# A sequential attention and GLU block on one core: two DMA writes swapped, a QKV tile and an empty background step moved in, transposes of the identity ahead of the first tile

## The chip, the cores and the metric

One core of a Trainium2 chip. The metric is the device time of one execution in microseconds (us), the median of the runs. The engines are named as the profile names them: PE is TensorE's matmul, PEld its weight load, DVE is VectorE, ACT is ScalarE, POOL is GpSimd, SP is SyncE; an engine's name with a q is its instruction queue, which issues DMAs.

## The reference

One sequence of 2048 tokens with 576 features passes a sliding, dilated attention (32 heads of 18, 8 keys at a distance of 2, only backwards) and a gated feed-forward layer, each behind a layer norm and with a residual.

```python
B, S, D, F = 1, 2048, 576, 4608
def attn(x, wqkv, wo):                       # H = 32, Dh = 18, W = 8, dil = 2
    q, k, v = split_heads(x @ wqkv)
    idx = pos[:, None] - arange(W) * dil
    logits = einsum("bhsd,bhswd->bhsw", q, k[idx]) * Dh ** -0.5   # idx < 0: -1e9
    o = einsum("bhsw,bhswd->bhsd", softmax(logits), v[idx])
    return o.reshape(B, S, D) @ wo
def glu(x, w_gate, w_up, w_down):
    return (sigmoid(x @ w_gate) * (x @ w_up)) @ w_down
h = x + attn(layernorm(x), wqkv, wo)
out = h + glu(layernorm(h), w_gate, w_up, w_down)
```

## The kernel before, in words

The tokens are split by parity and halves into four blocks (0 to 3) of 512 tokens, and each block into four tiles of 128. A matrix is held as a rounded part ("hi", made by ACT) and the remainder ("lo", made by DVE from the source and hi), and a product is three matmuls: hi by hi, lo by hi, hi by lo. `split` (lines 104 and 105) makes such a pair; `split_rest` (108 and 109) does it for the last 64 features, which lie twice in one 128-row chunk, so that one matmul takes both parts. Those doubled 64 columns are the "doubled rest": a row of normalised tokens or of attention output is 576 columns and the last 64 once more (`DX` = 640).

The work runs in this order.

- `opening()` takes block 0's first layer norm, its transposes and the QKV product of its first head group. Its instructions on each engine are chained by hand with `ch`: each stands behind the one before it on the same engine. `tr` (L497, L499) transposes a tile on PE by a matmul with the identity; `x_hi` (L504, L505) evicts it on ACT; `x_lo` (L509, L511) makes the remainder on DVE; `w_hi` and `w_lo` (L516, L519) do the same for the weights. `heads_of` runs one QKV tile, which is 14 matmuls of `tok_major` (L157, L159, L160). `qkv_w(1, ...)` splits the second group's weights (tile `qw`, L104 and L105).
- Then the QKV products of the blocks and groups follow on PE, while `att_all`, a generator that is stepped between them, runs the attention of blocks 0 and 1 on DVE (L189 to L226), group by group. Its results for block 0 stay on the chip (tile `tok`); L428 copies their last 64 columns. For other blocks ("spill") POOL writes them to DRAM tensors `o1` to `o3` (L228), and after the last of four groups also the doubled rest (L230), 64 columns for each of 512 tokens against 144 in L228.
- `front()` is block 0's output projection, residual, second layer norm and transposes. It is made of four generators `proj_j`, one a tile, and each `next(fr)` takes all four one step further. Step 1 is `tr_main` (L146) with a split, step 2 `tr_rest` (L150) with `split_rest`, steps 3 and 4 the two halves of the projection with the residual add (L262), then `ln_j` (L123 to L128), and the transposes of the result.
- The main loop runs over 84 items: 12 plain ones (`single`), 24 that take two blocks at once by a seven-product scheme (`pair`), then 12 and 36 for the other half of the tokens. Gate and up products are L746 and L753, down products L864 and L926. Weights come in by SP (L702, tile `wg`) and are split an item ahead (`weights`).
- Between the products of an item, a background generator is stepped by `bg_step`. In the first half it is block 1's projection, in the second the attention of blocks 2 and 3, their projections and the operands of the last pass. `proj_scr` runs such a projection: `load_j` (L707) loads a tile of attention output `oj` and of the input `hj`, then four `proj_j` are taken in turn, one step of one tile at a time, five rounds; their PSUM banks alternate between `b` and `bgp` (`bg_bank`). A plain item offers ten background steps in six places, two of them single and four double or single in turn.

The order on each engine comes from a planner that follows the order of the code, with priorities (`high_priority`). `tc.issue_after(x)` adds that what is issued in its block on x's own engine stands behind x; it sets nothing for other engines and adds no wait. Each engine runs its queue in order.

## Time and profile before

| | |
|---|---|
| runs | 1577.75 us (median), 1576.01 and 1581.7 |
| the profiled execution | 1584.01 us, span 1582.2 us |
| busy in the span | PE 1551.0, DVE 1255.2, ACT 879.2, POOL 199.9 us |
| granted TensorE clock, mean | 0.996 |
| HBM | 143.98 MB read, 130.87 MB written, 174 GB/s over the span |

In the profile's rows a line number is that of the kernel before. A row of a timeline has the start, the duration, the engine, the line, the operation, what it writes and reads, and in brackets the idle time of the engine before it and what ended it. A row of the waits has the total, the number and the longest, in us. Durations of matmuls overlap: the next one begins before the one before has drained. The chain that ended last runs for 58% of the span over PE, for 11% over DVE and for 8% over DMA.

### The profile page before, as it was taken

How to read it: one execution, taken by the hardware profiler on the slowest of the kernel's cores; microseconds unless marked ns; L12 is line 12 of the kernel's file. 1: busy time of each engine (PE TensorE's matmuls, PEld its weight loads, DVE VectorE, ACT ScalarE, POOL GpSimd, SP SyncE). 2: the span in 40 equal slices, each digit the busy share in tenths (PEclk: the TensorE clock that was granted, in tenths of full speed). 3: DMA queues.
4: the chain of work that ended last, by engine and by line, in shares of the span. 5: the costliest groups of instructions: out<-in, count | busy, mean ns of one | idle time of the engine just before them, and what ended most of it. 6: DMA issues, size and time to landing. Idle time of an engine off the chain costs nothing.

```text
span 1582.2 us, 22347 instructions
## 1 busy us (share of the span) xinstructions
PE 1551.0 (98%) x8520; PEld 1377.3 (87%) x8520; DVE 1255.2 (79%) x1883; ACT 879.2 (56%) x1584; POOL 199.9 (13%) x249
## 2 busy tenths in 40 slices
PE   8999999999999999999999999999999999999998
PEld 7999888887888888888888888888888888888887
DVE  6998999969999999999426588866777776677755
ACT  6632244435555645566542355766777766777660
POOL 2300000020000010000101010112112112111210
PEclk9999999999999999999999999999999999999999
DMA  8646445365566677664683524999899989999983
GB/s 284 215 168 220 179 185 190 108 235 183 133 167 170 164 176 192 157 162 109 161 242 125 181 81 126 193 181 177 170 180 186 173 173 181 173 173 186 181 169 120
DMA packets 77147, 273.95 MB, mean 173 GB/s; under 512 B 8336, under 2 KB 14224, under 8 KB 76144
## 3 DMA queue, kind: packets, MB, share of 16 engines
q0 software_dynamic: 28192, 107.29, 37.5%
q1 hardware_dynamic: 41216, 145.11, 27.2%
q10 hardware_dynamic: 7632, 20.12, 3.3%
q8 instruction: 66, 1.08, 0.3%
q14 instruction: 41, 0.34, 0.1%
HBM read 143.98 MB, written 130.87 MB: 174 GB/s over the span
## 4 chain that ended last, share of the span: by engine, by line
PE 58%; issue 16%; DVE 11%; DMA 8%; POOL 4%; ACT 2%; SPq 0%; ACTq 0%; POOLq 0%; DVEq 0%
PE b L746 27%; PE dp L864 13%; PE dp L926 6%; PE b L753 5%; PE acc L157 4%; POOL h L935 3%; DMA wg<-in_wmlp_dram 3%; DVE pr L189 2%; DVE pr L215 1%; DVE lg L193 1%; DVE w L105 1%; DVE pr L221 1%; PE b L157 1%; PE bgp L157 1%; DMA x<-tok 1%
## 5 line engine op out<-in xcount | busy, mean ns | idle before, releaser
L746 PE MATMUL b<-tl,w 128*128 128x512 f32 x1704 | 432.6, 393 | 5.1 <-ACT s L820 3.2
L746 PEld LDWEIGHTS b<-tl,w 128*128 128x128 f32 x1704 | 307.9, 188 | 63.6 <-ACT s L820 4.7
L746 PE MATMUL b<-th,w 128*128 128x512 f32 x1344 | 346.2, 392 | 1.5 <-DVE s L839 1.5
L746 PEld LDWEIGHTS b<-th,w 128*128 128x128 f32 x1344 | 244.8, 188 | 46.5 <-DVE s L839 1.9
L932 ACT ACTIVATE ev<-dp 128x576 f32<-128x576 f32 x224 | 144.7, 646 | 63.2 <-PE dp L926 58.9
L753 PE MATMUL b<-th,w 128*128 128x512 f32 x568 | 175.7, 390 | 0.0
L104 ACT ACTIVATE w<-wg 128x384 fp32r<-128x384 f32 (+1 forms) x186 | 110.8, 601 | 111.1 <-PE b L753 48.8
L935 POOL DMA_DIRECT2D h<-ev x128 | 110.0, 860 | 458.6 <-ACT ev L932 444.7
L157 PE MATMUL acc<-qw,th 128*128 128x432 f32 x512 | 154.3, 362 | 2.5 <-DVE th L109 2.3
L105 DVE TENSOR_TENSOR w<-wg,w 128x640 fp32r<-128x640 f32 (+1 forms) x186 | 120.8, 656 | 41.3 <-ACT w L104 41.1
L105 DVE TENSOR_TENSOR w<-tw,w 128x512 fp32r<-128x512 f32 x120 | 82.6, 688 | 82.1 <-ACT w L104 81.5
L753 PEld LDWEIGHTS b<-th,w 128*128 128x128 f32 x568 | 106.5, 188 | 23.2
L864 PE MATMUL dp<-d,h1h 128*128 128x288 f32 x640 | 119.9, 297 | 0.0
L864 PE MATMUL dp<-d,h0h 128*128 128x288 f32 x608 | 114.1, 297 | 0.8 <-DVE tail L874 0.8
L872 ACT ACTIVATE stage<-dp 128x576 f32<-128x576 f32 x104 | 66.9, 645 | 70.1 <-PE dp L864 69.8
L157 PEld LDWEIGHTS acc<-qw,th 128*128 128x128 f32 x512 | 96.6, 189 | 8.4 <-DVE th L109 3.5
L864 PEld LDWEIGHTS dp<-d,h1h 128*128 128x128 f32 x640 | 99.7, 190 | 3.0
L104 ACT ACTIVATE w<-tw 128x512 fp32r<-128x512 f32 x120 | 75.4, 628 | 46.5 <-PE b L746 40.0
L864 PEld LDWEIGHTS dp<-d,h0h 128*128 128x128 f32 x608 | 95.1, 190 | 4.3 <-DVE tail L874 1.0
L157 PE MATMUL acc<-qw,tl 128*128 128x432 f32 x256 | 92.6, 362 | 0.1
L189 DVE TENSOR_TENSOR pr<-kw,q 128x2304 f32<-128x2304 f32 x32 | 81.8, 2556 | 8.8 <-DMA kw<-k 8.7
L880 POOL DMA_DIRECT2D h<-stage x26 | 31.0, 1194 | 436.3 <-ACT stage L872 350.1
(310 smaller groups left out, 2955.5 us busy)
## 6 DMA issues: line engine op xcount, KB each, us to landing
h<-ev POOLq DMA_DIRECT2D x96, 576.0 KB, 7.1
wg<-in_wmlp_dram SPq DMA_DIRECT2D x47, 928.0 KB, 5.9
h<-stage POOLq DMA_DIRECT2D x26, 1152.0 KB, 9.5
wg<-in_wmlp_dram SPq DMA_DIRECT2D x36, 640.0 KB, 4.3
kw<-k SPq DMA_DIRECT2D x16, 792.0 KB, 5.2
vw<-v SPq DMA_DIRECT2D x16, 792.0 KB, 4.3
wd<-in_wmlp_dram SPq DMA_DIRECT2D x18, 576.0 KB, 7.4
h<-ev POOLq DMA_DIRECT2D x32, 288.0 KB, 6.9
```

The lines of the kernel that those rows point to most:

```text
L104: act.activation(hi, src, AF.Copy)
L105: splits.append(dve.tensor_tensor(lo, src, f32(hi), ALU.subtract))
L157: pe.matmul(ps[:, :n], a[:, c, js], m[:, c], start=k == 0, stop=False)
L189: dve.tensor_tensor(pr, both(kw, u), q[:, us].unsqueeze(2).broadcast_to([P, 2, W, CG]), ALU.mult)
L746: pe.matmul(ps, wt[:, a, k0 + c], xx[:, m + c], start=first and k == 0, stop=k == 5, skip_group_check=True)
L753: pe.matmul(ps, wt[:, a, k0], xx[:, 4], start=False, stop=a == 1, skip_group_check=True)
L864: pe.matmul(ps[:, i, :DH2], a[:, js], d[:, m, i * DH2:(i + 1) * DH2], start=k == 0, stop=k == n)
L872: act.activation(hv, ps, AF.Copy)
L880: pool.dma_start(hacc[b], hs, accum_op=ALU.add, max_dma_last_dim=8 * D)
L926: pe.matmul(ps[:, i, :DH2], a[x][:, js], m[y], start=k in (0, 1, 3) and q == 0, stop=q == 2, skip_group_check=True)
L932: act.activation(hs[:, k % 2], ps[:, :, :DH2], AF.Copy)
L935: pool.dma_start(hsev[:, u, k0:k + 1], hs[:, :k + 1 - k0], accum_op=ALU.add, max_dma_last_dim=8 * D)
```

## The change

Five places are edited.

1. In `attention`, POOL issues the write of the doubled rest ahead of the main write of the same group (last group of a spilled block only).
2. In `qkv_w(1, ...)`, ACT's casts stand behind tile 1's `x_hi` of the opening and DVE's remainders behind tile 1's `x_lo`. Before, one edge on a DVE instruction was given for both.
3. The opening begins with 20 transposes of the identity into a PSUM tile that nobody reads.
4. `front()`'s second step is taken after the third QKV tile of block 2's last group, together with the third step, and no longer right after the first.
5. In `proj_scr` for block 2, the generator yields once without work between the second and third tile of the first round. (A loop variable is renamed there.)

```diff
         if spill:
-            pool.dma_start(oscr[b][:, :, g * CG:(g + 1) * CG], o)
             if g == NG - 1:
                 pool.dma_start(oscr[b][:, :, D:DX], o[:, :, CG - DR:CG])
+            pool.dma_start(oscr[b][:, :, g * CG:(g + 1) * CG], o)
...
-            with ExitStack() as way:
-                way.enter_context(tc.high_priority(HI))
-                if after is not None:
-                    way.enter_context(tc.issue_after(getattr(after, "ins", after)))
-                split(w[:, 0, c], w[:, 1, c], ws)
+            with tc.high_priority(HI):
+                if after is None:
+                    split(w[:, 0, c], w[:, 1, c], ws)
+                    continue
+                x, y = (getattr(a, "ins", a) for a in after)
+                with tc.issue_after(x):
+                    act.activation(w[:, 0, c], ws, AF.Copy)
+                with tc.issue_after(y):
+                    dve.tensor_tensor(w[:, 1, c], ws, f32(w[:, 0, c]), ALU.subtract)
...
         nr, pv, pr = {}, {}, {}
+        pre = mm_tile()
+        for _ in range(20):
+            ch(pe, lambda: pe.transpose(pre[:, :P], ident, ident))
...
             ch(act, lambda: act.activation(th[:, 4, js], pr[j][:, :P], AF.Copy))
+            highs.append(last[act])
...
-    done = opening()
-    w.append(qkv_w(1, None, done[1]))
+    done, highs = opening()
+    w.append(qkv_w(1, None, (highs[1], done[1])))
...
     with tc.issue_after(getattr(last, "ins", last)):
-        for _ in range(2):
-            next(fr)
+        next(fr)
     for b in (2, 3):
         for j, _ in enumerate(more if b == 2 else qkv(b, 3, T[b], w[3])):
             with ExitStack() as way:
                 if (b, j) == (2, 0):
                     way.enter_context(tc.issue_after(getattr(passes[-1], "ins", passes[-1])))
+                    next(fr)
                 next(fr, END)
...
-        for _ in range(5):
-            for gn in live:
+        for k in range(5):
+            for j, gn in enumerate(live):
+                if b == 2 and (k, j) == (0, 2):
+                    yield
                 if todo and n % 2:
-                    j = todo.pop(0)
-                    ins[j][1] = load_j(pj, b, j, 1)
+                    i = todo.pop(0)
+                    ins[i][1] = load_j(pj, b, i, 1)
```

More of the change, by code (lines that the diff above doesn't have):

```diff
@@ L522, in opening @@
         call = qkv(0, 0, T[0], qw)
-        ends = []
+        ends, highs = [], []
         def heads_of(j):
@@ L564, in opening @@
         drain(call)
-        return ends
+        return ends, highs
     w = []
-    done = opening()
-    w.append(qkv_w(1, None, done[1]))
+    done, highs = opening()
+    w.append(qkv_w(1, None, (highs[1], done[1])))
     xb = load_x(1)
```

## The prediction

> **What bounds the kernel now.** I read the page first, then the table of waits of PE, then PE's and DVE's timelines around each long wait, and last a table of stretches for the granted clock.

> ```profile
> span 1582.2 us, 22347 instructions
> PE 1551.0 (98%) x8520; PEld 1377.3 (87%) x8520; DVE 1255.2 (79%) x1883; ACT 879.2 (56%) x1584; POOL 199.9 (13%) x249
> ```

> TensorE works in 98% of the span, so a microsecond is won only where TensorE waits or runs slowly; 1582.2 - 1551.0 leaves 31 us in all. The waits of PE between 180 and 1540 us that this change can touch:

> ```profile
> PE b L146 <- DMA oj<-o: 4.2, 1, 4.2
> ...
> PE b L146 <- DVE tl L105: 2.0, 1, 2.0
> PE mm L150 <- DVE tok L428: 1.7, 1, 1.7
> PE acc L157 <- DVE th L109: 1.6, 1, 1.6
> ```

> In order of time these are: block 0's projection (L428 and L109, near 180 us), block 1's projection (the load oj, at 315 us) and block 2's (L105, at 834 us). Two of them cost more than the wait. The stretches (length, then busy time of PE, PEld, DVE, ACT, POOL; the column after POOL is the granted clock):

> ```profile
> 3.65:14.07 10.42, 7.29 (x30) 5.62 (x30) 9.80 (x26) 7.64 (x18) 3.29 (x7) 1.00 0.97 348
> 181.25:207.20 25.95, 23.76 (x162) 22.96 (x162) 25.32 (x51) 4.66 (x12) 1.38 (x3) 1.00 0.34 134
> ...
> 314.31:317.72 3.41, 0.88 (x6) 0.56 (x4) 1.49 (x2) 1.79 (x3) 0.00 (x0) 1.00 0.18 16
> 317.72:324.55 6.83, 5.13 (x22) 5.08 (x23) 1.50 (x3) 1.55 (x3) 0.00 (x0) 0.50 0.97 364
> 389.40:392.82 3.42, 1.54 (x7) 0.94 (x5) 0.48 (x2) 2.29 (x5) 0.00 (x0) 1.00 0.01 4
> 392.82:396.23 3.41, 2.92 (x12) 2.17 (x12) 3.10 (x6) 2.57 (x5) 0.00 (x0) 1.00 0.00 0
> 833.14:836.55 3.41, 1.46 (x11) 1.09 (x10) 2.99 (x5) 2.83 (x6) 0.00 (x0) 1.00 0.34 83
> 836.55:839.96 3.41, 3.41 (x16) 3.41 (x15) 1.31 (x3) 1.33 (x2) 0.00 (x0) 0.50 0.99 394
> 940.00:1540.00 600.00, 600.00 (x3207) 523.51 (x3206) 440.00 (x757) 418.22 (x736) 111.26 (x129) 1.00 0.87 173
> ```

> After a 3.41 us stretch in which PE was busy for only 0.88 or 1.46 us, the next one or two stretches have half the clock; after one with 1.54 us busy they have not. So the 315 us wait costs 4.23 us and half of 5.13 us of slow work (2.57), and the 834 us wait 1.95 us and half of 3.41 us (1.71). From 940 to 1540 us PE never stops, so what is gained before stays gained.

> [...]

> **The opening: 20 transposes, and ACT's order.**

> ```profile
> 1.16 0.28 POOL masks.py:199 TENSOR_SCALAR_AFFINE_SELECT ident<-ident 128x128 f32<-128x128 f32 x1
> ...
> 6.59 1.12 PE L497 MATMUL mm<-ident,tok 128*128 128x128 f32 x4 [6.59 <-DVE tok L491]
> ...
> 9.78 0.29 ACT L505 ACTIVATE th<-acc 128x128 fp32r<-128x128 f32 x1
> ...
> 9.94 1.15 ACT L104 ACTIVATE qw<-ws 128x432 fp32r<-128x432 f32 x2
> ...
> 13.38 0.69 DVE L509 TENSOR_TENSOR tl<-mm,th 128x512 fp32r<-128x512 f32 x1
> ...
> 14.12 0.19 PEld L157 LDWEIGHTS acc<-qw,tl 128*128 128x128 f32 x1 [0.26 <-DVE tl L509]
> ```

> The identity is ready at 1.44 us. Four transposes take 1.12, so twenty take at most 5.6 and end by 7.0, at worst 0.45 us after the first real one now starts; that is the loss bound. The gain bound: PE works 7.29 us of the stretch up to 14.07, and if all of it ran at twice the speed it would save 3.6. But the work that releases PE at 14.12 is DVE's, and DVE is busy 9.80 of 10.42 us there, in an order fixed by hand (L509 of tile 0, weights, statistics, L509 of tile 1). A faster PE only waits longer for it. I take 0. What would be late without that cover is nothing else: it is DVE that covers. ACT's new edge asks that qw's casts (9.94) stand behind tile 1's x_hi (9.78 + 0.29); they stand there already. 0, with one answer.

> **The QKV tile between step 1 and step 2 of block 0's projection.**

> ```profile
> 181.25 0.49 DVE L428 COPY tok<-tok 128x64 f32<-128x64 f32 x4
> 181.79 0.33 PE L150 MATMUL mm<-ident,tok 128*128 128x128 f32 x1 [1.70 <-DVE tok L428]
> 185.30 0.46 PE L157 MATMUL acc<-qw,th 128*128 128x432 f32 x1 [1.65 <-DVE th L109]
> ...
> 209.36 0.33 PE L150 MATMUL mm<-ident,tok 128*128 128x128 f32 x1 [0.39 <-DVE tok L128]
> ```

> PE waits 1.70 for the copies and 1.65 for an accumulator bank that L109 must read. The moved tile of 14 matmuls fills both: 3.35 us on PE. But DVE works 25.32 of the 25.95 us to 207.20, and at 209.36 PE already waits for DVE's L128. If DVE is no earlier, the 3.35 us come back there as a longer wait, less the 0.39 that a shorter order may save. DVE gets earlier only by what it waits for PE on the way to block 1's attention:

> ```profile
> DVE s L766 <- PE b L753: 1.2, 1, 1.2
> ...
> DVE h L262 <- PE mm L160: 0.4, 1, 0.4
> DVE stage L874 <- PE dp L864: 0.3, 1, 0.3
> ```

> That is 1.9 us between 181 and 309 us. Ends: 0.4 and 3.35; I take 1.9.

> **The narrow write first.** It matters for block 1's last group alone; the two others are issued up to 753.9 us, for blocks whose transposes come after 830 (rows further down).

> ```profile
> L230 POOL DMA_DIRECT2D o<-kw x3: 817/838/842, 309.5 to 753.9; - x3
> 308.83 0.71 POOL L228 DMA_DIRECT2D o<-kw  x1 [43.26 <-DVE kw L226]
> 309.46 0.82 POOL L230 DMA_DIRECT2D o<-kw  x1
> DMA to landing us min/median/max: 4.5/4.5/4.5
> DMA to landing us min/median/max: 6.9/6.9/6.9
> 316.44 1.75 SPq L707 DMA_DIRECT2D oj<-o  x4
> 319.42 1.11 PE L146 MATMUL b<-ident,oj 128*128 128x128 f32 x4 [4.23 <-DMA oj<-o]
> ```

> The main write lands 4.5 us after its issue (313.3), the narrow one 6.9 after (316.3), and SP's loads leave at 316.44. Nothing but SP's loads stands behind the pair. After the change the main write is issued second, at 308.83 + 0.82 = 309.65. If it again takes 4.5 it lands at 314.1, 2.2 us earlier than now; if it takes the second place's 6.9, at 316.5, 0.2 later. I take its own row's 4.5 and add 0.82 for standing behind the narrow one's issue: 314.95, a gain of 1.36. PE then starts at 318.06 instead of 319.42. The stretch to 317.72 is still mostly idle, but the one after it is not, so the clock is back at 321.14: slow work of 3.08 us instead of 5.13, 1.03 less lost. Together 2.39; ends -0.2 and 2.2 + 2.57.

> [...]

> **The empty step in block 2.**

> ```profile
> 829.47 0.74 ACT L104 ACTIVATE w<-wg 128x640 fp32r<-128x640 f32 x1 [5.31 <-DMA wg<-in_wmlp_dram]
> ...
> 834.41 0.59 ACT L104 ACTIVATE th<-b 128x512 fp32r<-128x512 f32 x1
> ...
> 833.41 0.60 PE L146 MATMUL bgp<-ident,oj 128*128 128x128 f32 x4
> 835.96 0.66 PE L146 MATMUL b<-ident,oj 128*128 128x128 f32 x4 [1.95 <-DVE tl L105]
> 836.37 0.68 PE L864 MATMUL dp<-d,h1h 128*128 128x288 f32 x2
> ```

> Tile 2's transposes need the bank b that tile 0 holds; ACT evicts it only at 834.41, because a weight load kept ACT until 829.47 and its casts came first. With the empty step the down matmuls of L864, which start without a wait right behind, go ahead of tile 2, and the bank is free when they end. That removes 1.95 and the slow stretch, 1.71: 3.66. The price: all later steps of blocks 2 and 3 move one slot. Counted in the code, the background of this phase takes 98 of the 110 slots before the forced drain, so nothing is squeezed at its end; SP's loads stay inside the same item of the loop. But tile 0's rest now needs tile 2's bank one half product later, with ACT's next cast on a weight load perhaps ahead of it; that may give back up to 1.7. I take 3.66.

> **Sum.** 0 + 0 + 1.9 + 2.39 + 3.66 = 7.95 us off the profiled execution, which took 1584.01 us (span 1582.2): 1576.06. The median of the runs is 1577.75, a factor of 0.99605, so 1569.8. A measurement of this kernel tells about 0.5%, 7.9 us, from no change; the sum lies on that bound.

> **Rivals.**
> - B, DVE takes it back: PE waits for L128 as long as it gained, the writes' order is worth 0, and tile 0's rest gives back 1.7. 0.39 + 0 + 1.96 = 2.35: 1581.7, or 1575.4. For it: DVE's 25.32 of 25.95. Against it: DVE's own 1.9 us of waits for PE.
> - C, everything is kept: DVE's queue puts the small operations of the projection ahead of attention's, so 3.35 stays; the main write lands in 4.5, the wait at 315 falls to 2.0 us and straddles two stretches, so the clock stays up. 3.35 + 2.2 + 2.57 + 3.66 = 11.8: 1572.2, or 1566.0. For it: 1.54 us of work in a stretch was enough at 389. Against it: the new idle time could as well fall into one stretch.
> - E, the clock goes its own way: the two slow stretches are not due to these waits, or come back after other ones, and only the waits themselves are won. 1.9 + 1.36 + 1.95 = 5.2: 1578.8, or 1572.6. Against it: both slow stretches follow the two emptiest ones. [...]
> - D, slower: one slot later, a tile's eviction stands on ACT behind a cast that waits for its weight load. That wait was 5.31 at 829.47; PE then stops as long and loses, as at 315, 2.57 to the clock: 7.88, in block 2 and again in block 3's same step, 15.8, while 3.66 isn't had. 15.8 - 1.9 - 2.39 = +11.5: 1595.5, or 1589.2. It decides from 4.3 us of new waits, and beyond 0.5% from 12.2. Against it: a load that late occurs once in this stretch, and DVE and ACT have room.

> **How the numbers follow.** Forecast 0.38, of which 0.25 lies beyond 0.5% and 0.13 within, since half a microsecond in any term decides; C 0.27, faster; B 0.15 and E 0.05, within; D 0.15, slower. Faster 0.52, same 0.33, slower 0.15. The range leaves out D and the tails. Its low end is C's 1566.0 less the scatter of the runs below their median (1.74) and half the opening's bound (1.8): 1562.5. Its high end is B's 1575.4 plus the scatter above (3.95): 1579.4.

> **What would show it.** Right: no wait near 180 and 834 us and no half clock at 836; SP's oj loads 1 to 2 us sooner after DVE's last L226; PE's start at L157 near 14.1 unchanged. Wrong: L128's wait grown to 3 us; oj's loads still some 7.6 us after the POOL issue; a wait of L150 or L146 on ACT or DVE between 834 and 930; a different first attention start.

## The result, and the profile after

The changed kernel is slower: 1591.72 us (median of 6 runs, 1589.51 to 1595.25) against 1581.61 (6 runs, 1576.01 to 1582.81) of the kernel before, timed beside it. The ratio is 1.0068, with a 95% interval of 1.0052 to 1.0083. The forecast was 1569.8, faster.

The profiled execution after took 1591.32 us. Its line numbers have moved: L403 is now L407, L497 and L499 are L504 and L506, L702 is L710, L707 is L715, L746 and L753 are L754 and L761, L793 is L801, L820 is L828, L864 is L872. From the page, the span and the busy time:

```profile
span 1589.6 us, 22386 instructions
PE 1558.3 (98%) x8540; PEld 1383.2 (87%) x8540; DVE 1255.6 (79%) x1883; ACT 879.8 (55%) x1584; POOL 196.9 (12%) x249
```

PE is busy for 7.3 us more. The 20 transposes take about 4.5 of them, ahead of the first real work; the rest fits the slow work, since up to 1540 us the clock is half for 17.1 us, against 10.2 before. The waits of PE from 20 to 960 us (total, number, longest):

```profile
PE b L754 <- ACT s L828: 5.0, 3, 3.0
PE b L146 <- DMA oj<-o: 3.4, 1, 3.4
PE b L150 <- DVE tl L105: 3.0, 1, 3.0
PE b L754 <- ACT s L801: 2.5, 1, 2.5
PE bgp L146 <- DMA oj<-o: 1.9, 1, 1.9
PE acc L150 <- DVE tl L105: 1.6, 1, 1.6
PE acc L157 <- ACT ev L407: 1.5, 1, 1.5
```

The two waits that the change was to end, L150 on tok near 181 us (1.7) and L146 on tl at 834 (2.0), are gone. The second wait that the moved tile was to fill, L157 on th near 185 (1.6), has turned into one of L150 on tl (1.6, at 187). Beside it stand four that the kernel before did not have: L157 on ev (1.5, at 52 us), L754 on s of L801 (2.5, at 234), L150 on tl (3.0, at 846) and bgp on oj (1.9, at 893). The half clock has moved with them: it follows the wait at 234 and the old one at 394, while the 6.83 us behind the wait for oj are in both; the stretch from 832.98, where before had its wait, is full, and after the stretch with the new wait at 846 (1.55 us busy) the clock stayed up. The table of stretches (length, busy time of PE, PEld, DVE, ACT, POOL; behind POOL the granted clock):

```profile
232.49:235.90 3.41, 1.24 (x6) 0.69 (x4) 2.72 (x3) 0.97 (x2) 0.00 (x0) 1.00 1.05 439
235.90:239.31 3.41, 3.10 (x8) 2.63 (x9) 2.15 (x5) 3.26 (x7) 0.00 (x0) 0.50 0.10 42
...
392.91:396.33 3.42, 1.11 (x5) 0.57 (x4) 0.06 (x1) 2.06 (x4) 0.00 (x0) 1.00 0.02 7
396.33:403.15 6.82, 6.11 (x14) 4.81 (x15) 6.30 (x8) 3.45 (x7) 0.00 (x0) 0.50 0.00 0
832.98:836.39 3.41, 3.41 (x22) 3.08 (x21) 0.00 (x0) 0.00 (x0) 0.00 (x0) 1.00 1.05 363
846.88:850.29 3.41, 1.55 (x8) 1.31 (x9) 3.03 (x6) 1.24 (x4) 0.00 (x0) 1.00 0.40 155
```

How late PE is in the new trace at the same instruction of both (start after minus start before, same order of PE up to there):

| us before | 51 | 75 to 170 | 193 | 237 | 332 | 399 | 640 | 837 | 856 | 893 | 932 to 1540 |
|---|---|---|---|---|---|---|---|---|---|---|---|
| late by, us | 0.1 | 1.6 | 0.1 | 4.5 | 3.2 | 6.3 | 5.5 | 3.1 | 5.8 | 7.5 | 8.4 |

So the moved tile did win 1.5 us near 181, and the empty step 2 us at 834. Each is spent again within 60 us. The part at 394 is of another kind: the wait is in both traces (2.37 and 3.02), and no engine's order differs there.

The first explanation, from these traces and the order of each engine's program, was this. Outside the opening's hand-made chains, the order on every engine is the planner's own. An edit that moves one step changes the planner's estimate of when things are ready, and with that the order of instructions that the edit never named: loads on SP, casts on ACT, products on DVE. The four new waits come from four such changes (theory Q). The rival theory was that the loss belongs to the whole, by the phase of the clock's stretches or by edits that meet.

One caution holds for all that follows. Single executions of one program lie within about 11 us (of 127 runs of the kernel before, timed beside the experiments, 1576 to 1588), so a ledger of a single trace is good for places, not for totals. Totals are the ratios with their intervals.

### The profile page after: what moved, and what is told of

It reads as the page before. It is cut to its first block, busy times and chain, and to the rows that moved or that the text cites. A ratio compares the mean times of both kernels' runs of the same rounds, so it can differ in the third digit from the quotient of the medians.

```text
span 1589.6 us, 22386 instructions
## 1 busy us (share of the span) xinstructions
PE 1558.3 (98%) x8540; PEld 1383.2 (87%) x8540; DVE 1255.6 (79%) x1883; ACT 879.8 (55%) x1584; POOL 196.9 (12%) x249
## 4 chain that ended last, share of the span: by engine, by line
PE 59%; DVE 7%; issue 4%; DMA 4%; ACT 1%; POOL 1%; SPq 0%; POOLq 0%; DVEq 0%; ACTq 0%
PE b L754 32%; PE dp L934 11%; PE dp L872 9%; PE b L761 6%; DMA wg<-in_wmlp_dram 3%; DVE w L105 1%; DVE s L774 1%; DVE pr L215 1%; DMA oj<-o 0%; PE b L157 0%; DVE lg L193 0%; PE bgp L157 0%; DMA tail<-h 0%; DMA o<-kw 0%; ACT w L104 0%
## 5 line engine op out<-in xcount | busy, mean ns | idle before, releaser
L754 PE MATMUL b<-tl,w 128*128 128x512 f32 x1704 | 436.9, 396 | 8.0 <-ACT s L828 5.0
L754 PEld LDWEIGHTS b<-tl,w 128*128 128x128 f32 x1704 | 310.5, 190 | 66.9 <-ACT s L828 6.3
L754 PE MATMUL b<-th,w 128*128 128x512 f32 x1344 | 346.0, 392 | 0.9 <-DVE s L847 0.9
L754 PEld LDWEIGHTS b<-th,w 128*128 128x128 f32 x1344 | 245.1, 188 | 45.8 <-DVE s L847 1.3
L761 PE MATMUL b<-th,w 128*128 128x512 f32 x568 | 175.7, 390 | 0.0
L104 ACT ACTIVATE w<-wg 128x384 fp32r<-128x384 f32 (+1 forms) x186 | 111.1, 601 | 115.0 <-PE b L761 52.5
L157 PE MATMUL acc<-qw,th 128*128 128x432 f32 x512 | 154.4, 362 | 2.1 <-ACT ev L407 1.5
L105 DVE TENSOR_TENSOR w<-wg,w 128x640 fp32r<-128x640 f32 (+1 forms) x186 | 120.6, 653 | 44.7 <-ACT w L104 44.4
L105 DVE TENSOR_TENSOR w<-tw,w 128x512 fp32r<-128x512 f32 x120 | 82.2, 686 | 82.5 <-ACT w L104 81.8
L761 PEld LDWEIGHTS b<-th,w 128*128 128x128 f32 x568 | 106.6, 188 | 23.2
L872 PE MATMUL dp<-d,h1h 128*128 128x288 f32 x640 | 119.0, 295 | 0.0
L872 PE MATMUL dp<-d,h0h 128*128 128x288 f32 x608 | 114.4, 297 | 1.3 <-DVE tail L882 0.7
L157 PEld LDWEIGHTS acc<-qw,th 128*128 128x128 f32 x512 | 96.5, 189 | 7.9 <-ACT ev L407 1.7
L872 PEld LDWEIGHTS dp<-d,h1h 128*128 128x128 f32 x640 | 98.8, 189 | 3.0
L104 ACT ACTIVATE w<-tw 128x512 fp32r<-128x512 f32 x120 | 75.2, 628 | 46.5 <-PE b L754 36.4
L872 PEld LDWEIGHTS dp<-d,h0h 128*128 128x128 f32 x608 | 95.1, 190 | 5.1 <-DVE tail L882 0.9
L157 PE MATMUL acc<-qw,tl 128*128 128x432 f32 x256 | 92.4, 361 | 0.1
L189 DVE TENSOR_TENSOR pr<-kw,q 128x2304 f32<-128x2304 f32 x32 | 81.6, 2551 | 9.7 <-DMA kw<-k 9.5
## 6 DMA issues: line engine op xcount, KB each, us to landing
h<-stage POOLq DMA_DIRECT2D x26, 1152.0 KB, 10.2
```

Of the source, the lines that this page charges most:

```text
L104: act.activation(hi, src, AF.Copy)
L105: splits.append(dve.tensor_tensor(lo, src, f32(hi), ALU.subtract))
L157: pe.matmul(ps[:, :n], a[:, c, js], m[:, c], start=k == 0, stop=False)
L189: dve.tensor_tensor(pr, both(kw, u), q[:, us].unsqueeze(2).broadcast_to([P, 2, W, CG]), ALU.mult)
L754: pe.matmul(ps, wt[:, a, k0 + c], xx[:, m + c], start=first and k == 0, stop=k == 5, skip_group_check=True)
L761: pe.matmul(ps, wt[:, a, k0], xx[:, 4], start=False, stop=a == 1, skip_group_check=True)
```

## The experiments

### Each edit alone

The four kernels are before with one edit each, as in the diff of the change: the two writes swapped; the 20 transposes with the two edges; the moved second step; the empty step.

> Only the swap of the two POOL writes. Theory Q (the loss comes from orders that the planner changed on other queues, so this edit, which changes no queue but POOL's, loses nothing): the four-wide load of oj leaves SP about 6.8 us after the first write's issue and not 7.6, PE's wait at 315 us is 3.4 and not 4.23, the half clock behind it stays; -0.8 us, 1.000 of before within 0.2%. My prediction: -2.4 us with the clock back about 3 us sooner. Rival C (the loss belongs to the whole, through the phase of the clock's stretches): this alone may add a half-clock stretch near 391 us, where PE waits about 2.4 to 3.0 us, and cost about 2 to 3 us.

> Only the 20 transposes of the identity and the two separate edges of ACT and DVE in the opening. Theory Q: SP's queue in the opening is re-ordered, a load that waits for a buffer that L127 frees at 28.9 us stands ahead of the loads of q, kw and vw of the first attention, so the first L189 begins at 36.8 and not 35.05, DVE's first attention is 1.75 us later and PE is 1.6 us late from 52 us on; by PE's ledger +1.5 us from 52 to 175 us, then up to 1.5 of it given back where PE waited for DVE anyway: 0 to +1.7 at the end. PE's clock is full from 10.6 us as before. My prediction: 0, with the first L189 at 35.05. If the loss lies elsewhere: 0.

> Only the move of front()'s second step behind the third QKV tile. Theory Q: the wait at 181 us is gone and the one at 185 stays (about -1.5 us on PE), but DVE's order changes so that L226 ends 4 us later, SP's load of vw waits for its buffer until 223 and not 217 with the two wg loads right behind it in the queue, ACT's cast w<-wg waits about 4.8 us for its load and PE 2.5 us for s near 234 us, with half a clock for 3.4 us behind that: PE's ledger is about +3.5 us from 240 us on and +2.5 to +3.5 at the end. My prediction: -1.9 us. Rival: no more than +1, with the wait at 234 us absent, if that wait comes from edits together.

> Only the empty step between block 2's second and third tile. Theory Q: the wait of 1.95 us and the half clock at 834 us are gone (-3.7), but th<-b of tile 2 stands on ACT behind a cast that waits 2.9 us for wg, so PE waits about 3 us for L150 near 846, and the last oj load of block 3 stands on SP behind a wg load, so PE waits about 1.9 us near 893 and 0.7 near 936: +2 us, ledger 0 at 830, -3.7 at 838, -0.7 at 856, +1.2 at 895, +2 from 940 on. My prediction: -3.7 us. Rival D of the prediction: over +4.

| edit alone | ratio to before | 95% |
|---|---|---|
| writes swapped | 1.0008 | 0.9994 to 1.0022 |
| opening | 1.0006 | 0.9993 to 1.0018 |
| moved step | 1.0014 | 1.0000 to 1.0028 |
| empty step | 1.0026 | 1.0011 to 1.0041 |

No edit gains; the sum is 1.0054, and the whole has 1.0068 (1.0052 to 1.0083). The loss is the sum of the edits as far as these intervals reach, so the rival that needs them together is not needed. Each new wait appeared with its edit alone: 1.47 us at 54 with the opening, 2.63 at 232 with the moved step, 2.17 at 837 and 2.23 at 885 with the empty step. Theory Q was wrong on the swap: it expected the loads of oj 6.8 us after the first write's issue and 0.8 us won, and they leave 8.3 us after it.

**The swap.** In that kernel, POOL's writes and SP's loads, and the landing of both writes (288 KB is the main one, the last number is us from issue to landing):

```profile
310.38 0.71 POOL L229 DMA_DIRECT2D o<-kw  x1 [42.62 <-DVE kw L226]
311.01 0.82 POOL L230 DMA_DIRECT2D o<-kw  x1
318.68 1.75 SPq L707 DMA_DIRECT2D oj<-o  x4
o<-kw POOLq DMA_DIRECT2D x1, 288.0 KB, 7.5
o<-kw POOLq DMA_DIRECT2D x1, 128.0 KB, 4.0
```

The main write takes 4.5 us when it is first, but 7.5 as second (6.0 in the changed kernel). The loads leave 8.3 us after the first issue. Over all 18 profiles of this study they leave 6.1 to 7.6 us after it with the main write first (10 profiles, median 6.2) and 6.8 to 8.3 with the narrow one first (6 profiles, median 6.8). The gain of 0.8 read from the first pair of traces was the scatter of before's own 7.6, the longest of its ten.

**The moved step.** Rows of SP, ACT, PE and DVE in the kernel with that edit alone:

```profile
221.28 0.32 SPq L178 DMA_DIRECT2D vw<-v  x1
221.69 2.39 SPq L702 DMA_DIRECT2D wg<-in_wmlp_dram  x2
233.03 0.74 ACT L104 ACTIVATE w<-wg 128x640 fp32r<-128x640 f32 x1 [4.95 <-DMA wg<-in_wmlp_dram]
233.67 0.58 ACT L793 ACTIVATE s<-b 128x512 f32<-128x512 f32 x1
234.30 1.22 PE L746 MATMUL b<-tl,w 128*128 128x512 f32 x2 [2.63 <-ACT s L793]
...
276.88 2.55 DVE L189 TENSOR_TENSOR pr<-kw,q 128x2304 f32<-128x2304 f32 x1
279.35 0.68 DVE L766 TENSOR_TENSOR s<-s,b 128x512 f32<-128x512 f32 x1
280.75 0.53 PE L864 MATMUL dp<-d,h0h 128*128 128x288 f32 x2 [2.61 <-ACT h0h L104]
```

and DVE's two rows in the kernel before:

```profile
273.74 0.68 DVE L766 TENSOR_TENSOR s<-s,b 128x512 f32<-128x512 f32 x1
...
274.81 2.55 DVE L189 TENSOR_TENSOR pr<-kw,q 128x2304 f32<-128x2304 f32 x1
```

The chain reads from the top. DVE now takes the small operations of the projection ahead of the attention's, so the buffer that vw waits for is free 4 us later (vw left SP at 216.88 in before). The two weight loads wg stand behind vw on SP, as they did before: here it is DVE's order that changed, and SP's that hands the delay on. Their cast on ACT waits 4.95 us for them, and PE's bank b is evicted by the instruction behind that cast. A second change was found only here: at 276.88 DVE takes the 2.55 us product of the attention ahead of the 0.68 us product L766 that PE waits for; in before L766 came first.

### The opening's loads: a theory that fell

The first theory of the opening was that one load of block 3's x, which waits for its buffer, stood ahead of the loads of the first attention on SP.

```python
     xb = load_x(3, (0,))                                # was: load_x(3)
     with tc.issue_after(getattr(behind[0], "ins", behind[0])):   # the first attention's vw load
         load_x(3, (1, 2, 3), xb)
```

> The opening of the changed kernel (20 transposes, separate edges), with the last three of the four loads of block 3's x pinned on SP behind the loads of the first attention; nothing else changes on any queue. Theory Q (that load order is all that the opening costs): q leaves SP near 27.9 to 28.9 us and not 29.8 to 30.9, the first L189 begins near 35, PE's start after 52 us is that of before within 0.3 us where the kernel with the plain opening was 1.6 us late, and the mean of the runs falls from +1.6 us to 0 (within 1). Rival (the transposes or the casts' order on ACT cost it): still 1.6 us late at 52 us.

1.0019 (1.0006 to 1.0032), and PE waits 1.46 us for ev (L157) at 55 us as without the pin (1.47); from 75 us on it is 2.9 us late in this trace and 3.1 without the pin. The rows of SP show why:

```profile
29.59 0.35 SPq L345 DMA_DIRECT2D h<-in_x_dram  x1
...
30.45 0.42 SPq L176 DMA_DIRECT2D q<-q  x1
```

The first of the four loads, which stood ahead of q in before too, now leaves at 29.59 instead of 27.06. So everything is late already, and the order of those loads is a symptom. Going back along DVE and ACT leads to 15 us, shown here by the kernel with the plain opening:

```profile
15.26 1.31 SPq L378 DMA_DIRECT2D wr<-in_wqkv_dram  x3
16.67 0.38 SPq L386 DMA_DIRECT2D ws<-in_wqkv_dram  x1
...
17.62 0.38 SPq L386 DMA_DIRECT2D ws<-in_wqkv_dram  x1
...
20.94 0.56 ACT L395 ACTIVATE qw<-ws 128x432 fp32r<-128x432 f32 x1 [2.72 <-DMA ws<-in_wqkv_dram]
...
38.19 2.56 DVE L189 TENSOR_TENSOR pr<-kw,q 128x2304 f32<-128x2304 f32 x1 [4.51 <-DMA kw<-k]
```

Three loads of the next group's weights (wr) now stand ahead of the last two weight pieces (ws) of the group that is wanted at once. In before the pieces came first:

```profile
16.79 0.35 SPq L386 DMA_DIRECT2D ws<-in_wqkv_dram  x1
...
19.09 3.40 SPq L378 DMA_DIRECT2D wr<-in_wqkv_dram  x5
```

ACT's cast waits 2.72 us instead of 0.72, DVE's remainder and the layer norm queued behind it come 2 to 3 us later, and the first attention 3.1 (35.05 before). DVE is busy for 257.4 of the 271.8 us from there to 310, so it catches up slowly: POOL's write of its last product for block 1 still leaves 1.2 us later than before.

The second try pins wr, and the zero writes of groups 2 and 3, behind the last ws:

```python
     with tc.issue_after(behind[0]):                     # the last ws load of qkv_w(1)
         wr = raw_w(2)
```

> The opening of the changed kernel (20 transposes, separate edges), with the loads of group 2's weights wr and the zero writes of groups 2 and 3 pinned on SP behind the last weight piece ws of group 1. Theory Q2 (the opening's cost is that the two last ws pieces stand on SP behind a zero write and three wr loads, so that ACT's cast and DVE's layer norm behind it come 1.5 to 2 us later): ws leaves SP within 0.8 us of 15.06 and 16.79, ACT's wait for ws near 20 us falls from 2.48 to about 0.7, the first L189 begins near 35 to 35.5, PE after 52 us is late by 0.3 us and not by 1.5; the mean of the runs is that of before within 1 us, and 2 to 3 us under the plain opening's. Rival (the transposes themselves or ACT's order): 1.5 us late at 52 us still.

0.9997 (0.9983 to 1.0012), with all 20 transposes in it.

```profile
16.95 0.33 SPq L386 DMA_DIRECT2D ws<-in_wqkv_dram  x1
...
20.33 0.56 ACT L396 ACTIVATE qw<-ws 128x432 fp32r<-128x432 f32 x1 [1.51 <-DMA ws<-in_wqkv_dram]
35.62 2.56 DVE L189 TENSOR_TENSOR pr<-kw,q 128x2304 f32<-128x2304 f32 x1 [3.57 <-DMA kw<-k]
```

PE's wait for ev is down to 0.33 us, and PE is 0.5 us late behind it. The cast still waits 1.51 us, where 0.7 was expected. The opening's price on PE was SP's order; the transposes themselves cost and give nothing that these runs can tell. Whether the transposes or the two edges made the planner re-order SP was not tried apart. In five of the nine profiles that have the transposes the first full clock is recorded at 5.2 to 7.4 us instead of 10.5 to 10.7, and in those, too, PE was no earlier at 20 us: DVE covers it, as predicted.

### The wg load ahead of vw

The moved step again, with vw of block 1's third group loaded one stage later, behind the first wg load:

```python
             if (b, g) != (1, 2): sp.dma_start(vw..., window(vscr[e][g], hf))
     ...     # after the first L193 of that group:
             if (b, g, u) == (1, 2, 0): paced(vw..., window(vscr[e][g], hf))
```

> The moved second step of front(), and the load of vw for the attention of block 1's third group issued later, so that the first wg load of the main loop stands ahead of it on SP. Theory Q: the wg load no longer waits for the slot of vw, ACT's cast w<-wg waits under 1 us near 230, PE's wait of 2.5 us at 232 and the half clock behind it are gone, and the 2 us won at 181 stay on PE's ledger from 190 to 310 us: -1 to -2 us against before there, and over 3 us better than the tile's move alone; at the end -1.5 to 0. Rival (the wait at 232 comes from ACT's own order or from DVE, not from the load): it stays at 2 us or more.

```profile
227.81 0.72 ACT L104 ACTIVATE w<-wg 128x640 fp32r<-128x640 f32 x1
228.44 0.58 ACT L797 ACTIVATE s<-b 128x512 f32<-128x512 f32 x1
...
233.56 1.20 PE L750 MATMUL b<-tl,w 128*128 128x512 f32 x4 [1.35 <-DVE w L105]
...
277.10 0.69 PE L868 MATMUL dp<-d,h0h 128*128 128x288 f32 x2 [1.76 <-ACT h0h L104]
```

The cast has no wait, and PE waits 1.35 us, now for DVE, with a full clock behind it. That part of the wait is DVE's order again: with the moved step a 2.55 us product of the attention (L189 in before, here L190 at 230.22) stands ahead of the remainder that PE needs (L105, at 232.69), and in before it stood behind. In all four profiles with this mend that wait is 1.33 to 1.35, and 2.5 to 2.6 in the five with the moved step and no mend. But the runs are no better: 1.0026 (1.0009 to 1.0044) against 1.0014 without the mend. The wait at 276 stayed (1.76 here; 0.4 to 2.7 in the nine profiles with the moved step, at most 0.9 without it). What the single runs hide was asked again inside the whole change, below.

### A second empty step, and both given back

The empty step again, with another one ahead of the first rest of the second round, and two steps in one slot twice in the third round:

```python
                 if b == 2 and (k, j) in ((0, 2), (1, 0)):
                     yield
...
                 next(gn)
                 if b != 2 or (k, j) not in ((2, 0), (2, 2)):
                     yield
```

> The empty step in block 2, a second empty step ahead of the first rest of the second round, and both slots given back in the third round (two steps in one slot, twice), so that the last oj load of block 3 stays ahead of the wg load on SP. Theory Q: no wait at 834; the first L150 finds its bank free, so no wait of 2 to 3 us near 838 to 846; the wait of 1.9 to 2.2 us for oj near 885 to 893 gone; PE's ledger -2 to -3.7 us against before from 860 on, and the mean of the runs about 2 us under before and 5 us under the empty step alone. Rival (any shift of these steps costs as much as it gains): waits of over 2 us in the sum appear between 834 and 900, and no gain.

First the kernel with the plain empty step, ACT, PE and SP:

```profile
835.85 0.74 ACT L104 ACTIVATE w<-wg 128x640 fp32r<-128x640 f32 x1 [2.89 <-DMA wg<-in_wmlp_dram]
836.49 0.58 ACT L104 ACTIVATE th<-b 128x512 fp32r<-128x512 f32 x1
838.76 0.33 PE L150 MATMUL b<-ident,oj 128*128 128x128 f32 x1 [2.17 <-DVE tl L105]
...
878.50 0.33 SPq L702 DMA_DIRECT2D wg<-in_wmlp_dram  x1
879.55 0.33 SPq L707 DMA_DIRECT2D oj<-o  x1
887.11 0.63 PE L146 MATMUL bgp<-ident,oj 128*128 128x128 f32 x4 [2.23 <-DMA oj<-o]
```

Tile 2's eviction (th at 836.49) stands behind a cast that waits 2.89 us for its load, and tile 0's rest needs that bank: rival D's mechanism. Fifty microseconds later one wg load has slipped ahead of the last oj. With the mend:

```profile
839.11 0.74 ACT L104 ACTIVATE w<-wg 128x640 fp32r<-128x640 f32 x1 [3.06 <-DMA wg<-in_wmlp_dram]
...
842.03 0.33 PE L150 MATMUL b<-ident,oj 128*128 128x128 f32 x1 [0.65 <-DVE tl L105]
...
878.18 0.33 SPq L707 DMA_DIRECT2D oj<-o  x1
...
879.07 0.38 SPq L702 DMA_DIRECT2D wg<-in_wmlp_dram  x1
```

ACT still waits as long, but PE has other work until the bank is free (0.65), oj is ahead of wg again, and the waits at 834 and 885 are gone. 0.9996 (0.9984 to 1.0008), against 1.0026 for the plain empty step. In the runs the gain expected against before (2 us) is not told from zero.

### The mended parts together

The mended empty step and the mended moved step:

> The two mended edits together (the moved step with the wg load first, and two empty steps given back), without the swapped writes and without the opening's edits. Theory Q: the sum of the two, -2 to -5 us against before (1574 to 1577 where before is 1579), the first version here that beats it. Rival (edits together meet in a new wait or in the phase of the clock): no better than before.

1.0006 (0.9993 to 1.0020): no better than before, so the rival's outcome; the moved step still costs what it wins (a wait of 2.67 at 276). Then all five edits, each with its mend, the swap as it is:

> All five edits, each with its mend: the ws pieces first in the opening, the first wg load ahead of vw, the two empty steps given back. Theory Q2: the change's loss of 10 us shrinks to what is not mended, the swap of the writes (about +1) and the moved tile (about +1 to +3): +1 to +4 us against before, 6 to 9 us under the change as given; no wait over 2 us at 845 and 893. Rival (the loss belongs to the edits together): still +7 or more.

1.0006 (0.9990 to 1.0022), the low end of what theory Q2 expected. The loss of 1.0068 is all but gone with three orders put right and no edit taken back. No wait of PE between 800 and 960 us is over 0.5 us.

### One mend at a time inside the whole change

> The whole change with only the opening's mend (ws pieces ahead of wr and of the later zero writes). The change as given stands at 1.0068 of before. If the parts add up, the opening's share of 2 to 3 us goes: 1.0045 to 1.0055; PE is 0.3 us late after 52 us and not 1.5. If the loss belongs to the combination: 1.0068 still.

> The whole change with only the first wg load put ahead of vw. By the traces the wait at 232 us falls from 2.5 to 1.35 and the half clock behind it goes (2.9 us in the sum); by the pair of single runs, 1.0014 without and 1.0026 with that mend, it is worth nothing. Expected 1.0050 to 1.0068; I take 1.0060.

> The whole change with only the second empty step and the two slots given back. By the single runs (1.0026 against 0.9996) this is the largest share, 4.7 us: 1.0030 to 1.0045, with no wait over 2 us between 834 and 940. If the loss belongs to the combination: 1.0068 still.

> The whole change without the swap of the two writes. By the profiles the first oj load leaves SP 6.1 to 7.6 us (median 6.3) after the first write's issue and with the swap 6.8 to 8.3: worth 0.5 to 1 us, 1.0060 to 1.0068, about what can be told at all. If the swap is worth what the prediction said (2.4 us won), this is slower than the whole change: 1.0083.

| the whole change | ratio to before | 95% |
|---|---|---|
| as given | 1.0068 | 1.0052 to 1.0083 |
| opening mended | 1.0040 | 1.0021 to 1.0058 |
| wg ahead of vw | 1.0048 | 1.0028 to 1.0069 |
| empty step mended | 1.0034 | 1.0017 to 1.0051 |
| without the swap | 1.0053 | 1.0033 to 1.0074 |

All four lie below the whole, by 2.8, 2.0, 3.4 and 1.5 parts in a thousand; each difference has an uncertainty of about 2.5, and the kernel as given was timed apart from the four, beside its own before. So the empty step is the largest share and the opening the next; the two others are not told from zero one by one. The three mends together took away 6.2 (from 1.0068 to 1.0006), where the sum of the three alone is 8.2: within that uncertainty they add up.

The 18 profiles tell the shares apart better than the runs do. Over the stretch that an edit bears on, this is by how much PE's lateness against the trace of before grows, as a mean (in brackets the number of profiles and their range; the two kernels with a write on ACT's queue, which come next, are not in the swap's row):

| stretch, us | without the edit | with it, as given | with its mend |
|---|---|---|---|
| opening, 0 to 172 | -0.1 (9; -0.8 to 0.6) | 2.8 (6; 1.6 to 3.5) | -0.5 (3; -1.4 to 0.7) |
| moved step, 172 to 300 | -0.2 (9; -2.4 to 3.4) | 3.0 (5; 1.2 to 5.5) | 1.3 (4; 0.7 to 1.9) |
| swap, 300 to 345 | -1.8 (10; -3.7 to 0) | -1.3 (6; -2.9 to 0.1) | |
| empty step, 820 to 940 | 0.2 (8; -1.4 to 1.8) | 3.6 (5; 2.3 to 4.9) | -2.3 (5; -2.8 to -1.2) |

As given less without, the four are 2.9, 3.2, 0.5 and 3.4 us, together about the 10 us of the medians. For the opening and the empty step the ranges as given and without do not meet; the moved step is shown by its mean alone, and the swap is not told from zero. The mended empty step gains 2.5 us in its stretch, as was expected of it.

### The writes on two queues, and the best version

```python
             (act if b == 1 else pool).dma_start(oscr[b][:, :, D:DX], o[:, :, CG - DR:CG])
```

> Before, with the narrow write of block 1's doubled rest issued on ACT's queue instead of POOL's. Theory W (the second of two writes in POOL's queue is what comes late, whichever it is: 5.3 to 7.5 us against 3.8 to 4.7 for the first): both land about 4.0 to 4.7 us after their issues, the first load of oj leaves SP about 5.0 to 5.4 us after the first issue and not 6.1 to 7.6 (eight profiles) or 6.8 and 8.3 (the swapped order), PE's wait at 315 us shortens by 1 to 1.5 us; the run -0.5 to -2 us. Rival (the narrow write's 512 short rows are slow by themselves, or the two share the memory): it lands 5.5 us or later on its own queue too, and nothing is won.

```profile
o<-kw POOLq DMA_DIRECT2D x1, 288.0 KB, 5.5
o<-kw ACTq DMA_DIRECT2D x1, 128.0 KB, 2.4
...
313.08 2.71 SPq L707 DMA_DIRECT2D oj<-o  x4
```

On its own queue the narrow write lands 2.4 us after its issue, not 5.3 to 6.9. So its 512 short rows did not make it late. The place behind the other write did for the larger part, but not alone: as the first of two in POOL's queue it took 3.7 to 4.2. And the main write now takes 5.5 instead of 4.5; what of the narrow one still bears on it was not shown. The loads leave 5.8 us after the first issue, 0.4 us sooner than the median. PE waits 2.3 us for the first tile of oj, against 2.8 to 4.2 with both writes on POOL and the main one first, and then 1.0 more for the next tile. The time is unchanged, 1.0006 (0.9991 to 1.0021); theory W is right on the queue and too large in its price.

> The narrow write on ACT's queue and the two empty steps given back, the two parts that theories W and Q support, and nothing else of the change. Expected -2 to -4 us against before (0.9975 to 0.9987): 1 to 1.5 and its share of the clock at 315, 2 to 3 at 834. If the gains at single places are taken back later: no difference.

0.9987 (0.9973 to 1.0001), median 1579.1 against 1579.64: the fastest version here. It beats the changed kernel; against before the interval just reaches 1, and as the lowest of 17 ratios it may owe a part to luck.

## Why the prediction was wrong

The sign was wrong. What the change wins directly was seen rightly at two places; what it moves elsewhere was priced at nothing. Term by term:

- **The opening, 0.** That DVE covers the transposes holds: PE is no earlier behind them (0.1 us late at 51 us). The step that failed is "with one answer": the new edge was looked up on ACT alone. SP was not counted among the queues that the planner would re-order. It is a wait of 1.5 us at 54 us in all six profiles with the edit as given, 1.6 to 3.5 us on PE's ledger behind it, and 2.8 parts in a thousand inside the whole.
- **The moved tile, -1.9.** It won 1.2 to 2.2 us on PE's ledger near 192 in eight of the nine profiles that have it (0.3 in the ninth, which has a half clock there). Three of the nine without it have a half clock there too, so on the mean its win is 2.2. That this is the size forecast is partly luck: the tile filled one of the two waits, not both, and the second came back as 1.0 to 2.1 us on tl. But the rival that DVE takes it back was looked for at L128 only. The step that failed is that nothing else would be late. The gain goes back by the wg load behind vw and a remainder behind L189 (2.5 at 234, with half a clock behind it in four of five profiles) and by L766 behind L189 (0.4 to 2.7 at 276). The queues behind the moved step were not followed further, to 300 us.
- **The narrow write, -2.39.** The term that failed is the landing: I gave the main write in second place its 4.5 us of the first place plus 0.82. It takes 6.0 to 7.5. Of the two bounds I gave (4.5 and 6.9), the far one was right, and the swap costs about 0.6 us. Rival B's 0 for the order of the writes is a term that no run shows; the profiles show loads that leave 6.2 us after the first issue with the main write first and 6.8 with the narrow one (medians). That is nearer to B's 0 than to my term.
- **The empty step, -3.66.** The 1.95 us did go. The 1.71 of half clock was no fixed cost: in the profiles with the edit absent the wait at 834 was 1.75 to 3.35 us, and the half clock followed it in five of eight. "SP's loads stay inside the same item of the loop" failed at 885 (1.7 to 2.6 us in five profiles), and rival D's mechanism, a tile's eviction behind a cast that waits for its load, took 2.2 to 3.0 at 840 in the same five. I had priced D from the 5.31 us wait at 829 and set it in block 2 and block 3 alike; it is 2 to 3 us, once, with the oj load as its second half. That made D look like an unlikely 15.8 us, where a likely 5 was enough to turn the sign of this edit.
- **The sum.** -7.95 forecast, +8.4 in the profile from 932 us on, +10.1 by the medians. Rival D was the only case of the right sign, with a chance of 0.15. Its time, 1589.2, is near the measured 1591.7, but for half of its reason only.

Right were: no wait near 181 on tok and none at 834; no earlier start of PE behind the opening; and what the prediction had listed as signs of its failure, a wait of L150 on DVE between 834 and 930, and a later first attention.

What stays open: what the runs, and not the profiles, would give as the shares of the four side effects, since their intervals are about as wide as they are; which part of the opening's edit re-ordered SP; and whether the moved step could win with DVE's order at 230 and 276 put right, which was not tried.

## What to carry to other kernels

Where a planner orders the queues, an edit's price is read from the order of every queue before and after, SP's first: count the loads that have changed places or whose buffer comes free later, and ask for each which cast waits for it and what stands behind that cast. A step that is moved into a wait wins that wait only if the slot is given back nearby; left shifted, it slips past loads that nobody meant to touch. And a wait that one trace shows ought to be seen in a second one before it is priced: here the one trace, with the loads 7.6 us after the first write's issue, was the longest of ten.
